# First attention of an attention, gated MLP and attention chain: P of the last sixteen couples of groups turned in blocks on VectorE and put in place through DRAM

## The chip, the cores and the metric

One core of one Trainium2 chip. The time is device time of one launch in microseconds (us), the median of three runs. Engines: PE (TensorE), DVE (VectorE), ACT (ScalarE), POOL (GpSimd) and SP (SyncE, which issues the DMAs here).

## What is computed

Four sequences of 576 positions, fp32 throughout. A first attention (8 heads of 64, a causal window of 64 positions) is followed by a gated MLP (512 to 1024 to 512 with a matmul over positions in the middle), and that by a second, causal attention with four heads, of which a gate picks two per position.

```python
def _attn_ref(q, k, v):                       # q, k, v: (4, 8, 576, 64)
    scores = scale * np.matmul(q, k.transpose(0, 1, 3, 2))
    rel = pos[:, None] - pos[None, :]
    scores = np.where((rel >= 0) & (rel < 64), scores, -1000000000.0)
    attn = np.exp(scores - np.max(scores, axis=-1, keepdims=True))
    attn = attn / (np.sum(attn, axis=-1, keepdims=True) + 1e-09)
    return np.matmul(attn, v)

def _moe_ref(x, w_in, w_spatial, b_spatial, w_out):
    h = np.maximum(x @ w_in, 0.0)
    u, v = h[..., :512], h[..., 512:]
    v_n = (v - mu) / np.sqrt(var + 1e-06)     # over the last axis
    v_s = np.einsum('ts,bsd->btd', w_spatial, v_n) + b_spatial[None, :, None]
    return (u * v_s) @ w_out

def _moe2_ref(x, w_gate, wq, wk, wv, wo):     # four heads, causal
    out += mask[..., None] * w[:, :, kk:kk + 1] * (a @ v @ wo[e])
```

## The kernel before, in words

The program is written out by a planner. The kernel's functions make nodes, each with an engine, a planned duration, what it depends on, which ring slots it takes and which it uses; a node's priority is its entry in the hand-kept list KEY (2089 numbers, in the order in which nodes are made). `Planner.run` (line 224 on) then plays the machine forward: whenever an engine is free, of the nodes that are ready and have room in their rings it starts the one with the lowest priority number, and issues its instructions there and then. So the order on each engine, SP's DMA queue included, is fixed when the program is built, from planned durations. What PE does has a form: 0 for full-size matmuls and transposes, 1 for the scores of the first attention (64x64 pieces of the array), 2 for P times V, 3 for the second attention's scores. Taking a node of form 0 after another form, or the other way round, adds SWITCH to its number in the choice (line 252), and DRAIN (line 187) to its planned time.

There are two stages with one `plan.run()` each. The first makes the first attention and the MLP of all four sequences and folds the MLP's last weight into the weights of the second attention (q, k, v). The second is the second attention.

*The first attention* works in groups: one sequence, one pair of heads, one third of the positions (192). There are 48 groups, taken two at a time by `a_couple(n0)` (24 couples, n0 = 0, 2, ... 46). For one couple:

- SP loads q of each group into a ring of six (`load_q`), and k and v once per pair of heads (`load_kv`). All loads, and the stores of the output, go through `dma` (line 509) onto SP's queue, which takes them strictly in order.
- `s_mm` (form 1): 12 fp32 matmuls (24 instructions) put the scores of three tiles of 64 queries into two PSUM banks, one for each head of the pair; a tile is 128 rows (64 queries of each of the two groups) by 128 keys.
- For each of the two banks: `s_top` (line 629, DVE) adds the mask, scales and takes the row extreme, writing to a tile `pa`; `s_exp` (line 635, ACT) exponentiates; a reduce and a reciprocal (lines 651 and 653, DVE) give 1/sum; `s_norm` (lines 641 on ACT, 643 on DVE or POOL) multiplies; `p_t` (line 647, PE) makes three 128x128 transposes into a PSUM bank; a copy (line 427 on ACT, 431 on DVE) brings them to a tile `pt`. `pa` and `pt` have four buffers each, of one bank's size.
- `pv` (form 2): 12 fp32 matmuls (24 instructions) of v with P from `pt` give the attention's output for both groups in one bank, from which ACT and DVE make a high and a low part (`xh`, `xl`), the operands of the following matmuls in the faster fp32r format. There are six `xh` and six `xl`; a sequence takes four.

*The MLP* of sequence b: `b_v` (V, five pieces of the positions), `b_u` (U, eight pieces), `b_mix` (eight pieces, 14 matmuls each: the matmul over positions). V of a sequence needs `xh` and `xl` of all its heads. While sequence b goes through the MLP, the attention of sequence b+1 is made (`weave`).

*Fillers.* At the start PE has to wait for loads; 60 matmuls of the identity with itself (FILL, `heat`) are nodes of the lowest priority, so they are placed in the first stage wherever nothing else is ready.

*The second attention* (`unit`, line 1278) has its own P, multiplied at line 1317 by DVE or POOL and transposed on PE at line 1329; the change leaves its operations as they are. Every matmul of the program is issued in `mm` (line 416), every copy in `copy` (427 to 431), every subtraction of a high part in `sub` (440).

Of the kernel before, what the change touches and what calls it, by code (L numbers as in the profile page):

```python
# [22 lines left out]
N_XT = 5  # L23
N_VR = 3
N_W2 = 2
N_Q = 6
SWITCH = (51316.5562883, 56444.76665)
A_BIAS = 10098.0
C_BIAS = 162315.0
DVE_BIAS = (924.812225719, 2809.18155958)  # L30
POOL_BIAS = (605.73769693, 3223.06614942)
# [3 lines left out]
EFT = (348.130120865, 591.3127716)  # L35
# [6 lines left out]
    1e+09, 1e+09, 1e+09, 1e+09, 1e+09, 1e+09, 1e+09, 1e+09, 1e+09, 1e+09, 1e+09, 1e+09, 1e+09, -433949.337, -310768.212, -410360.675, -53326.873, -46012.043, -29718.587, 29893.476, 36423.798, 130640.442, 48760.892, -102410.634,  # L42
# [309 lines left out]
def attn_gmlp_moe_kernel(ctx: ExitStack, tc: tile.TileContext, kq0, qT, kT, v, w_in, wspT, b_sp, w_outT,  # L352
# [228 lines left out]
    def a_couple(n0):  # L581
# [42 lines left out]
        for ps, pt in zip(bank, pts):  # L624
# [8 lines left out]
            def s_exp(_, pa=pa, mx=mx):  # L633
                for j in range(3):
                    act.activation(pa[:, j, :], pa[:, j, :], AF.Exp, bias=mx[:, j, 0:1], scale=-1.0,  # L635
                                   accum_out=mx[:, j, 1:2])
# [880 lines left out]
```

## Time and profile before

| what | value |
|---|---|
| runs | 441.45, 441.62, 443.12 us; median 441.62 us |
| the profiled execution | 441.42 us, of which its span (first to last instruction) 439.6 us |
| TensorE clock granted | full (1.00) over the span |
| first stage | to about 258 us |
| instructions | 10921 |
| moved by DMA | 33.11 MB, of which 27.68 MB read from HBM and 4.72 MB written |

The profile is one execution, recorded by the hardware. Busy time of an engine is the time in which an instruction of it was running; matmuls are pipelined, so the duration of one overlaps the next, and what one costs PE is the distance between starts. "Idle before" is the time in which the engine stood before a group's instructions, with what ended it (the releaser). The chain that ended last is followed back from the last instruction, at each step to what released it or to the instruction before it on its engine.

### The profile page before, as it was taken

The numbers are of one execution on the slowest core, as the hardware profiler recorded it, in microseconds if no ns is written. First come the engines' busy times: TensorE is split into PE (matmuls) and PEld (weight loads), VectorE is DVE, ScalarE is ACT, GpSimd is POOL, SyncE is SP. The second block draws the span as 40 slices with busy tenths as digits, with TensorE's granted clock in tenths as the row PEclk, the third lists the DMA queues.
The fourth block names the chain that finished last, engine by engine and source line by source line (L and its number), as shares of the span: only waits on it lengthen the run. The fifth ranks groups of instructions, "written<-read, shape, count | busy, mean of one in ns | idle before, by whom it ended". The sixth has DMA issues, their size and how long they took to land.

```text
span 439.6 us, 10921 instructions
## 1 busy us (share of the span) xinstructions
PE 432.1 (98%) x4058; PEld 390.0 (89%) x4058; DVE 288.6 (66%) x1238; ACT 275.8 (63%) x883; POOL 90.0 (20%) x132
## 2 busy tenths in 40 slices
PE   8999999999999999999999999999999999999997
PEld 7988989998889989998999999999799978987775
DVE  4999998695787583354435444977654956498750
ACT  4899986787785273352433352867576748557873
POOL 4556754121041050001100120120012101110000
PEclk9999999999999999999999999999999999999999
DMA  8995614364145020121001000000020002000114
GB/s 269 339 343 151 238 51 154 96 205 120 38 108 147 1 73 0 49 73 49 1 1 50 0 1 1 0 2 2 1 97 1 1 1 98 1 0 2 49 51 143
DMA packets 31079, 33.11 MB, mean 75 GB/s; under 512 B 1905, under 2 KB 24689, under 8 KB 31026
## 3 DMA queue, kind: packets, MB, share of 16 engines
q1 hardware_dynamic: 31026, 32.41, 23.5%
q8 instruction: 32, 0.52, 0.5%
q14 instruction: 21, 0.17, 0.1%
HBM read 27.68 MB, written 4.72 MB: 74 GB/s over the span
## 4 chain that ended last, share of the span: by engine, by line
PE 84%; DVE 10%; ACT 3%; issue 1%; DMA 1%; POOL 1%; SPq 0%; DVEq 0%; POOLq 0%; ACTq 0%
PE bank L416 75%; PE bank L1329 5%; PE bank L647 4%; DVE p L1307 3%; DVE p L1300 2%; DVE p L1317 1%; ACT p L1313 1%; DMA kt<-in_kT_dram 1%; POOL p L1317 1%; DVE mc L1315 1%; DVE qk L440 0%; DVE mc L1316 0%; ACT pa L635 0%; DVE t2w L440 0%; DVE pa L629 0%
## 5 line engine op out<-in xcount | busy, mean ns | idle before, releaser
L416 PE MATMUL bank<-xh,w 128*128 128x288 f32 x512 | 109.5, 298 | 0.0
L416 PEld LDWEIGHTS bank<-xh,w 128*128 128x128 f32 x512 | 84.1, 188 | 1.4 <-issue 0.3
L416 PE MATMUL bank<-xl,w 128*128 128x288 f32 x256 | 75.5, 295 | 0.0
L416 PE MATMUL bank<-w,xh 128*128 128x512 f32 (+1 forms) x256 | 64.8, 343 | 0.0
L635 ACT ACTIVATE pa<-pa,mx 128x128 f32<-128x128 f32 x144 | 55.8, 393 | 12.7 <-DVE mx L629 12.6
L1313 ACT ACTIVATE p<-p,mc 128x256 f32<-128x256 f32 (+4 forms) x72 | 41.5, 577 | 15.5 <-DVE mc L1307 13.7
L416 PEld LDWEIGHTS bank<-xl,w 128*128 128x128 f32 x256 | 48.1, 188 | 0.4
L416 PEld LDWEIGHTS bank<-w,xh 128*128 128x128 f32 x256 | 43.0, 188 | 5.0 <-DVE mx L651 0.2
L416 PE MATMUL bank<-w,xl 128*128 128x512 f32 (+1 forms) x128 | 43.2, 338 | 0.0
L1317 POOL TENSOR_SCALAR p<-p,mc,fx 128x384 f32<-128x384 f32 (+4 forms) x22 | 14.6, 664 | 133.8 <-DVE mc L1316 66.8
L416 PE MATMUL bank<-wsp_h,vh 128*128 128x288 f32 x128 | 38.9, 304 | 0.0
L416 PE MATMUL bank<-wsp_l,vh 128*128 128x288 f32 x128 | 37.7, 294 | 0.0
L416 PE MATMUL bank<-wsp_h,vl 128*128 128x288 f32 x128 | 37.7, 294 | 0.0
L1307 DVE CUSTOM_DVE_ANT_0 p<-bank,cmask 128x512 f32<-128x512 f32 (+3 forms) x64 | 28.8, 487 | 4.8 <-PE bank L416 2.4
L629 DVE CUSTOM_DVE_ANT_0 pa<-bank,mask 128x128 f32<-128x128 f32 x120 | 28.2, 286 | 4.4 <-PE bank L416 4.3
L853 POOL TENSOR_TENSOR st<-st,nhalf 128x1 f32<-128x1 f32 (+1 forms) x20 | 11.8, 592 | 92.2 <-DVE st L852 56.6
L427 ACT ACTIVATE pg<-bank 128x512 f32<-128x512 f32 (+4 forms) x80 | 29.7, 438 | 0.7 <-PE bank L1329 0.2
L1329 PE MATMUL bank<-ident,p 128*128 128x128 f32 x192 | 27.2, 276 | 1.7 <-DVE p L1317 0.7
L427 ACT ACTIVATE pt<-bank 128x384 f32<-128x384 f32 x41 | 18.4, 486 | 15.8 <-PE bank L647 15.8
L635 ACT ACTIVATION_READ_ACCUMULATOR pa<-pa,mx 128x1 f32 x144 | 27.6, 192 | 0.0
L416 PEld LDWEIGHTS bank<-w,xl 128*128 128x128 f32 x128 | 24.1, 188 | 2.8
L1329 PEld LDWEIGHTS bank<-ident,p 128*128 128x128 f32 x192 | 21.6, 140 | 5.5 <-DVE p L1317 2.6
(193 smaller groups left out, 989.9 us busy)
## 6 DMA issues: line engine op xcount, KB each, us to landing
vt<-in_v_dram SPq DMA_DIRECT2D x12, 512.0 KB, 5.0
qa<-in_qT_dram SPq DMA_DIRECT2D x44, 96.0 KB, 4.4
out_dram<-ot SPq DMA_DIRECT2D x15, 256.0 KB, 2.1
y<-in_w_in_dram SPq DMA_DIRECT2D x7, 512.0 KB, 6.2
kt<-in_kT_dram SPq DMA_DIRECT2D x12, 288.0 KB, 5.3
y<-in_w_outT_dram SPq DMA_DIRECT2D x4, 512.0 KB, 4.2
y<-in_wspT_dram SPq DMA_DIRECT2D x2, 576.0 KB, 4.0
vt<-in_kq_dram SPq DMA_DIRECT2D x2, 384.0 KB, 3.8
```

What stands on the lines that cost most here:

```text
L416: pe.matmul(o, lhsT, rhs, start=start, stop=stop)
L427: act.activation(o, i, AF.Copy)
L629: dve.tensor_tensor_reduce(out=pa[:, j, :], in0=ps[:, j * 128:(j + 1) * 128], in1=mask(j), scale=-0.125, scalar=3.0e38, op0=ALU.add, op1=A ...
L635: act.activation(pa[:, j, :], pa[:, j, :], AF.Exp, bias=mx[:, j, 0:1], scale=-1.0, accum_out=mx[:, j, 1:2])
L647: pe.transpose(ps2[:, j * 128:(j + 1) * 128], pa[:, j, :], ident)
L853: a = N((POOL, 464), lambda e: pool.tensor_tensor(out=st[:m, 9:10], in0=st[:m, 8:9], in1=nhalf[:m], op=ALU.pow), [n1], use=[st])
L1300: dve.tensor_tensor_reduce(out=P[HALF[y], a0:a1], in0=ps[y][HALF[y], :HS], in1=cmask[HALF[y], 0:HS] if i == 0 else tmask[HALF[y]], scale=- ...
L1307: tops = [N((DVE, t_tt(L)), lambda _, ps=ps: dve.tensor_tensor_reduce(out=P[:, cs], in0=ps[:, cs], in1=cmask[:, 512 - L:512], scale=-0.125 ...
L1313: a = N((ACT, 284 + 0.87 * L), lambda e: act.activation(P[:, cs], P[:, cs], AF.Exp, bias=mc[:, 0:1], scale=-1.0, accum_out=mc[:, 2:3]), to ...
L1315: a = N((DVE, 70), lambda e: dve.tensor_scalar(mc[:, 3:4], mc[:, 2:3], 1e-9, None, op0=ALU.add), [a], use=[mc], prio=prio)
L1317: a = N({POOL: 328 + 0.832 * L, DVE: 90 + 0.52 * L}, lambda e: engs[e].tensor_scalar(P[:, cs], P[:, cs], mc[:, 3:4], fx[:, I, ev:ev + 1], ...
L1329: pe.transpose(ps[:, j * m:(j + 1) * m], P[:, c0 + j * 128:c0 + (j + 1) * 128], ident)
```

## The change

`N_DT = 16` splits the couples. Those with n0 below 16 (eight couples) keep the way described above. For the other sixteen:

- `s_top`, `s_exp` and `s_norm` write `pa` in another order of columns: four blocks of 32 keys, in each both heads, the three tiles and 32 keys. `pa` now holds both banks of a couple (768 columns, four buffers).
- `p_t` and the copies out of PSUM are not made. Instead one DVE instruction, `dve.transpose` of 128x768 in place, turns each block of 32x32; it waits for the norms of both banks.
- Four DMAs, one for each 32 partitions (98 KB), store the result to a DRAM tile `dr` (a ring of four). One DMA of 393 KB, after all four have landed, loads it with the blocks in place into `pt` (768 columns, three buffers). Both move rows of 192 numbers (768 bytes). All are on SP's queue.
- `pv` reads P from `pt` in two runs of 32 columns.

Beside that, PE's planned times of forms 1 and 2 are without the cost of the form change, which is now in the table DRAIN, with a form 4 of its own for transposes; SWITCH multiplies DRAIN in the choice instead of standing alone; the biases (DVE_BIAS, POOL_BIAS, EFT) and one planned time of the second stage (line 1317 on DVE) are other numbers. Per changed couple four nodes go and three come, so KEY has 2073 entries instead of 2089, and all but the first 61 (the warm-up and the fillers) are new numbers. FILL stays at 60. The list KEY is left out here:

```diff
+N_DT = 16
...
-SWITCH = (51316.5562883, 56444.76665)
+SWITCH = (508440.848706, 1241.9455123)
 A_BIAS = 10098.0
 C_BIAS = 162315.0
-DVE_BIAS = (924.812225719, 2809.18155958)
-POOL_BIAS = (605.73769693, 3223.06614942)
+DVE_BIAS = (1446.55002243, 5820.53335932)
+POOL_BIAS = (791.503455194, 4103.69459824)
...
 WARM = 8
 FILL = 60
...
-EFT = (348.130120865, 591.3127716)
+EFT = (590.178157957, 3173.43987937)
...
-    DRAIN = (0.0, 145.0, 145.0, 92.0), (0.0, -78.0, 0.0, 0.0), (0.0, 0.0, -78.0, 0.0), (0.0, 0.0, 0.0, -92.0)
+    DRAIN = ((0.0, 138.0, 137.0, 191.0, 0.0),
+             (212.0, 0.0, 158.0, 212.0, 165.0),
+             (204.0, 151.0, 0.0, 204.0, 157.0),
+             (194.0, 141.0, 140.0, 0.0, 147.0),
+             (0.0, 145.0, 144.0, 198.0, 0.0))
...
-                    key = n.prio + (SWITCH[self.phase] if e == PE and (n.form > 0) != (self.form > 0) else 0.0), n.nth
+                    key = n.prio + (SWITCH[self.phase] * self.DRAIN[self.form][n.form] if e == PE else 0.0), n.nth
...
+    dram = ctx.enter_context(tc.tile_pool(name="dram", bufs=1, space=bass.MemoryType.DRAM))
...
-    r_pa = ring(p1, "pa", [128, 3, 128], F32, 4)
+    r_pa = ring(p1, "pa", [128, 768], F32, 4)
 
     r_mx = fixed(MX)
-    r_pt = ring(p1, "pt", [128, 3, 128], F32, 4)
+    r_pt = ring(p1, "pt", [128, 768], F32, 3)
+    r_dr = ring(dram, "dr", [4, 4, 32, 192], F32, 4)
...
-        pts = [r_pt.new(), r_pt.new()]
+        far = n0 >= N_DT
+        pa, pt = r_pa.new(), r_pt.new()
+
+        def at(j, e):
+            if far:
+                return pa.t.rearrange("p (k e j c) -> p k e j c", k=4, e=2, j=3)[:, :, e, j, :]
+            return pa[:, e * 384 + j * 128:e * 384 + (j + 1) * 128]
+
+        def sq(x):
+            return x.rearrange("p (k c) -> p k c", c=32) if far else x
+
+        def prob(j, x, e):
+            if far:
+                return pt.t.rearrange("p (i e j c) -> p i e j c", i=4, e=2, j=3)[:, 2 * x:2 * x + 2, e, j, :]
+            return pt[:, e * 384 + j * 128 + x * 64:e * 384 + j * 128 + x * 64 + 64]
...
-        S_N[n0] = S_N[n0 + 1] = top = N((PE, 816), s_mm, kn + [Q_N[n0], Q_N[n0 + 1], S_N.get(n0 - 1)], alloc=bank, use=hk, prio=prio,
+        S_N[n0] = S_N[n0 + 1] = top = N((PE, 654), s_mm, kn + [Q_N[n0], Q_N[n0 + 1], S_N.get(n0 - 1)], alloc=bank, use=hk, prio=prio,
                                         form=1)
-        done = []
-        for ps, pt in zip(bank, pts):
-            pa, mx, ps2 = r_pa.new(), r_mx.new(), r_at.new()
-
-            def s_top(_, ps=ps, pa=pa, mx=mx):
+        done, first, turned = [], [], []
+        for e2, ps in enumerate(bank):
+            mx = r_mx.new()
+
+            def s_top(_, ps=ps, e2=e2, mx=mx):
                 for j in range(3):
-                    dve.tensor_tensor_reduce(out=pa[:, j, :], in0=ps[:, j * 128:(j + 1) * 128],
-                                             in1=mask(j), scale=-0.125, scalar=3.0e38,
+                    dve.tensor_tensor_reduce(out=at(j, e2), in0=sq(ps[:, j * 128:(j + 1) * 128]),
+                                             in1=sq(mask(j)), scale=-0.125, scalar=3.0e38,
                                              op0=ALU.add, op1=ALU.min, accum_out=mx[:, j, 0:1])
 
-            def s_exp(_, pa=pa, mx=mx):
+            def s_exp(_, e2=e2, mx=mx):
                 for j in range(3):
-                    act.activation(pa[:, j, :], pa[:, j, :], AF.Exp, bias=mx[:, j, 0:1], scale=-1.0,
+                    act.activation(at(j, e2), at(j, e2), AF.Exp, bias=mx[:, j, 0:1], scale=-1.0,
                                    accum_out=mx[:, j, 1:2])
 
-            def s_norm(e, pa=pa, mx=mx):
+            def s_norm(e, e2=e2, mx=mx):
                 if e == ACT:
                     for j in range(3):
-                        act.activation(pa[:, j, :], pa[:, j, :], AF.Copy, scale=mx[:, j, 3:4])
+                        act.activation(at(j, e2), at(j, e2), AF.Copy, scale=mx[:, j, 3:4])
+                elif far:
+                    o = pa.t.rearrange("p (k e j c) -> p k e j c", k=4, e=2, j=3)[:, :, e2]
+                    engs[e].tensor_tensor(out=o, in0=o, in1=mx[:, None, :, 3:4].to_broadcast([128, 4, 3, 32]), op=ALU.mult)
                 else:
-                    engs[e].tensor_tensor(out=pa.t, in0=pa.t, in1=mx[:, :, 3:4].to_broadcast([128, 3, 128]), op=ALU.mult)
-
-            def p_t(_, pa=pa, ps2=ps2):
-                for j in range(3):
-                    pe.transpose(ps2[:, j * 128:(j + 1) * 128], pa[:, j, :], ident)
-
-            a = N((DVE, 606), s_top, [top], alloc=[pa, mx], use=[ps], prio=prio)
+                    o = pa[:, e2 * 384:(e2 + 1) * 384].rearrange("p (j c) -> p j c", j=3)
+                    engs[e].tensor_tensor(out=o, in0=o, in1=mx[:, :, 3:4].to_broadcast([128, 3, 128]), op=ALU.mult)
+
+            a = N((DVE, 606), s_top, [top] + first, alloc=[mx] + ([] if e2 else [pa]), use=[ps] + ([pa] if e2 else []), prio=prio)
+            first.append(a)
             a = N((ACT, 1160), s_exp, [a], use=[pa, mx], prio=prio)
             a = N((DVE, 75), lambda e, mx=mx: dve.tensor_reduce(out=mx[:, :, 3], in_=mx[:, :, 1:3], axis=AX.X, op=ALU.add),
                   [a], use=[mx], prio=prio)
             a = N((DVE, 91), lambda e, mx=mx: dve.reciprocal(mx[:, :, 3], mx[:, :, 3]), [a], use=[mx], prio=prio)
             a = N({POOL: 1053, DVE: 450, ACT: 880}, s_norm, [a], use=[pa, mx], prio=prio, sbuf=True)
-            a = N((PE, 327), p_t, [a], alloc=[ps2, pt], use=[pa], prio=prio)
-            done.append(N(on_copy(384), lambda e, pt=pt, ps2=ps2: copy(e, pt.t.rearrange("p a b -> p (a b)"), ps2[:, :384]),
+            if far:
+                done.append(a)
+                continue
+            ps2 = r_at.new()
+
+            def p_t(_, e2=e2, ps2=ps2):
+                for j in range(3):
+                    pe.transpose(ps2[:, j * 128:(j + 1) * 128], at(j, e2), ident)
+
+            a = N((PE, 327), p_t, [a] + turned, alloc=[ps2] + ([] if e2 else [pt]), use=[pa] + ([pt] if e2 else []), prio=prio, form=4)
+            turned.append(a)
+            done.append(N(on_copy(384), lambda e, e2=e2, ps2=ps2: copy(e, pt[:, e2 * 384:(e2 + 1) * 384], ps2[:, :384]),
                           [a], use=[ps2, pt], prio=prio))
+        if far:
+            a = N((DVE, 870), lambda e: dve.transpose(pa.t, pa.t), done, use=[pa], prio=prio, sbuf=True)
+            dr = r_dr.new()
+
+            def there():
+                for i in range(4):
+                    dma(dr[i].rearrange("k a w -> a k w"), pa[i * 32:(i + 1) * 32, :].rearrange("p (k w) -> p k w", k=4))
+
+            a = load(128 * 3072, 4, there, [a], alloc=[dr], use=[pa], prio=prio)
+            done = [load(128 * 3072, 1, lambda: dma(pt.t.rearrange("p (i w) -> p i w", i=4),
+                                                    dr.t.rearrange("i k a w -> (k a) i w")), [a], alloc=[pt], use=[dr], prio=prio)]
...
-                        mm(ps3[HALF[e], (3 * x + j) * 64:(3 * x + j + 1) * 64], vap(x, vi, e), pts[e][:, j, HALF[x]])
+                        mm(ps3[HALF[e], (3 * x + j) * 64:(3 * x + j + 1) * 64], vap(x, vi, e), prob(j, x, e))
...
-        o = N((PE, 848), pv, done + [PV_N.get(k[:2]) for k in grp] + vn, alloc=[ps3] + new, use=pts + hv, prio=prio,
+        o = N((PE, 699), pv, done + [PV_N.get(k[:2]) for k in grp] + vn, alloc=[ps3] + new, use=[pt] + hv, prio=prio,
...
-        a = N({POOL: 328 + 0.832 * L, DVE: 90 + 0.52 * L}, lambda e: engs[e].tensor_scalar(
+        a = N({POOL: 328 + 0.832 * L, DVE: 190 + 0.52 * L}, lambda e: engs[e].tensor_scalar(
...
-    nc = _bacc.Bacc("TRN2", target_bir_lowering=False, num_devices=1)
+    nc = _bacc.Bacc("TRN2", target_bir_lowering=False, num_devices=1, dynamic_dma_scratch_size=2048)
```

## Rows read from the trace of the kernel before

**Rows 1.** The page's first part: busy time, share of the span, instructions.

```profile
PE 432.1 (98%) x4058; PEld 390.0 (89%) x4058; DVE 288.6 (66%) x1238; ACT 275.8 (63%) x883; POOL 90.0 (20%) x132
```

**Rows 2.** Busy time by stage: us, each engine, clock, DMA share, GB/s.

```profile
28.00:66.00 38.00, 37.00 (x444) 32.42 (x446) 35.35 (x133) 35.93 (x115) 24.53 (x26) 1.00 0.52 175
66.00:100.00 34.00, 34.00 (x413) 32.03 (x406) 27.58 (x138) 25.69 (x104) 9.97 (x12) 1.00 0.48 147
100.00:150.00 50.00, 50.00 (x546) 44.97 (x545) 34.33 (x159) 32.04 (x121) 8.98 (x13) 1.00 0.33 91
150.00:200.00 50.00, 50.00 (x506) 46.29 (x505) 26.80 (x99) 25.30 (x82) 7.27 (x8) 1.00 0.15 43
```

**Rows 3.** The chain that ended last, merged, in order: start, duration in us.

```profile
60.16 15.97 PE bank L416 x190
76.13 1.31 PE bank L647 x12
...
196.21 0.33 PE bank L647 x3
196.53 77.48 PE bank L416 x592
```

**Rows 4.** PE's timeline at the ninth couple's scores: start, duration in us.

```profile
42.38 0.89 PE L416 MATMUL bank<-kt,qa 64*64 64x128 f32 x24
```

**Rows 5.** Groups of instructions by shape, copies of P: busy us, mean ns.

```profile
L427 ACT ACTIVATE pt<-bank 128x384 f32<-128x384 f32 x41 | 18.4, 486 | 15.8 <-PE bank L647 15.8
...
L431 DVE COPY pt<-bank 128x384 f32<-128x384 f32 x7 | 3.8, 545 | 0.0
```

**Rows 6.** The same view, DVE from SBUF to SBUF.

```profile
L440 DVE TENSOR_TENSOR xl<-y,xh 128x576 fp32r<-128x576 f32 x10 | 7.9, 813 | 3.6 <-ACT xh L427 3.4
...
L1317 DVE TENSOR_SCALAR p<-p,mc,fx 128x576 f32<-128x576 f32 x7 | 4.0, 578 | 0.1
...
L440 DVE TENSOR_TENSOR w<-vt,w 128x1024 fp32r<-128x1024 f32 x3 | 3.7, 1226 | 1.1 <-ACT w L427 0.9
```

**Rows 7.** DMA: queue and issues, 66 to 200 us; the page's stores.

```profile
q1 hardware_dynamic: 16206, 11.47, 29.4%
...
L509 SPq DMA_DIRECT2D qa<-in_qT_dram x23: 327/423/1668, 67.4 to 132.5; - x23
...
DMA to landing us min/median/max: 1.9/4.1/6.8
...
out_dram<-ot SPq DMA_DIRECT2D x6, 128.0 KB, 2.3
```

**Rows 8.** ACT's timeline, the last exp of two couples: start, duration in us.

```profile
142.81 0.19 ACT L635 ACTIVATION_READ_ACCUMULATOR pa<-pa,mx 128x1 f32 x1
...
192.36 0.19 ACT L635 ACTIVATION_READ_ACCUMULATOR pa<-pa,mx 128x1 f32 x1
```

**Rows 9.** PE's timeline, blocks of PV and what follows them.

```profile
87.64 0.92 PE L416 MATMUL bank<-pt,vt 128*64 128x64 f32 x24
88.48 0.89 PE L416 MATMUL bank<-kt,qa 64*64 64x128 f32 x24
...
177.64 1.62 PE L416 MATMUL bank<-pt,vt 128*64 128x64 f32 x48
179.19 0.40 PE L416 MATMUL bank<-wsp_h,vh 128*128 128x288 f32 x1
...
198.31 0.92 PE L416 MATMUL bank<-pt,vt 128*64 128x64 f32 x24
```

**Rows 10.** PE's timeline, fillers at the end of the first stage.

```profile
256.02 2.84 PE L416 MATMUL bank<-ident 128*128 128x128 f32 x24
```

**Rows 11.** Waits of PE's weight loads: total us, times, longest.

```profile
PEld bank L1329 <- DVE p L1317: 2.6, 7, 0.7
PEld bank L1329 <- POOL p L1317: 1.5, 4, 0.6
```

More of the change, by code (lines that the diff above doesn't have):

```diff
@@ L41 @@
     1e+09, 1e+09, 1e+09, 1e+09, 1e+09, 1e+09, 1e+09, 1e+09, 1e+09, 1e+09, 1e+09, 1e+09, 1e+09, 1e+09, 1e+09, 1e+09, 1e+09, 1e+09, 1e+09, 1e+09, 1e+09, 1e+09, 1e+09, 1e+09,
-    1e+09, 1e+09, 1e+09, 1e+09, 1e+09, 1e+09, 1e+09, 1e+09, 1e+09, 1e+09, 1e+09, 1e+09, 1e+09, -433949.337, -310768.212, -410360.675, -53326.873, -46012.043, -29718.587, 29893.476, 36423.798, 130640.442, 48760.892, -102410.634,
[85 rows of a table removed]
+    1e+09, 1e+09, 1e+09, 1e+09, 1e+09, 1e+09, 1e+09, 1e+09, 1e+09, 1e+09, 1e+09, 1e+09, 1e+09, -1183064.921, -1180401.788, -984440.607, -770425.267, -965452.953, -700022.553, -767274.631, -735858.745, -731589.461, -769196.477, -803420.559,
[84 rows of a table added]
 )
@@ L914, in gv @@
         def gv(g):
-            return g.t.rearrange("p a b -> p (a b)")[:, :HS]
+            return g[:, :HS]
         def gate(o):
@@ L1253, in scores @@
                 ps = [r_sc.new(), r_sc.new()]
-                a = N((PE, 92 + 3 * t_mm(HS)), lambda _, ps=ps, i=i: three(
+                a = N((PE, 3 * t_mm(HS)), lambda _, ps=ps, i=i: three(
                     [p[:, :HS] for p in ps], (S - 64, S - 128), i * HS, (i + 1) * HS),
@@ L1269, in go @@
                 c += w
-        a = N((PE, 92 + sum(3 * t_mm(128 * I + 128) for I in tiles)), go, deps, alloc=ps + pp + gets, use=[qk], prio=prio, form=3)
+        a = N((PE, sum(3 * t_mm(128 * I + 128) for I in tiles)), go, deps, alloc=ps + pp + gets, use=[qk], prio=prio, form=3)
         started(a)
@@ L1336, in unit @@
         f, an = a, PG_N[key][:1]
-        a = N((PE, nj * 109), tr, [f] + an, alloc=[ps], use=[P], prio=prio)
+        a = N((PE, nj * 109), tr, [f] + an, alloc=[ps], use=[P], prio=prio, form=4)
         a = N(on_copy(nj * m, 1), tc_, [a], use=[ps, pg], prio=prio)
@@ L1344, in unit @@
             a = N((PE, 109), lambda _: pe.transpose(pt[:64, :128], P[:, 512:576], ident), [f] + PG_N[key][:1], alloc=[pt],
-                  use=[P], prio=prio)
+                  use=[P], prio=prio, form=4)
             a = N(on_copy(128), lambda e_: copy(e_, pg[HALF[hb], 3, :, 64 * hb:64 * hb + 64],
@@ L1372, in c_pv @@
         cs = slice(i0, i0 + 256)
-        o = N((PE, 800 if grp == 0 else 2200), go, PG_N[b, pr, grp] + V2_N[b] + (VT_N[b] if grp else []) + ([] if new else O_N[b, pr][:1]),
+        o = N((PE, 651 if grp == 0 else 2056), go, PG_N[b, pr, grp] + V2_N[b] + (VT_N[b] if grp else []) + ([] if new else O_N[b, pr][:1]),
               alloc=[ps] + new, use=[pg, v2] + ([vt] if grp else []), prio=prio, form=2)
@@ L1417, in c_wo @@
             return
-        a = N((PE, 78 + 6 * t_mm(512)), lambda e: mm3(ps.t, [
+        a = N((PE, 6 * t_mm(512)), lambda e: mm3(ps.t, [
             ((part(0, pr), part(1, pr)), (view(wh.t)[:, pr, :], view(wl.t)[:, pr, :])) for pr in range(2)]),
```

169 rows, old and new, of the table KEY are left out of this document.

## The prediction

> **What bounds the kernel now.** I read the page first, then the stages, then the chain that ended last. PE is busy 98% of the span, the other engines 20 to 66% [rows 1]. The mean hides where a second engine is close: from 28 to 66 us DVE works 35.35 of 38 us, from 66 to 200 us 88.7 of 134 us (27.58 + 34.33 + 26.80), while PE has no idle time that the rows show after 66 us [rows 2]. The chain says what this means: from 60.16 us to 274 us it holds nothing but PE, line 416 (all matmuls) and line 647 (the transposes of P) by turns [rows 3]. In that stretch a microsecond taken from PE is a microsecond of the kernel, as long as nothing else comes late. Before 60 us the chain also runs through DMA, ACT and DVE, and there the change removes nothing: the eight couples that keep their transposes are scored up to 41 us, and the ninth, the first that changes, at 42.38 us [rows 4].
>
> **The change, part by part.**
>
> *Transposes off PE.* Sixteen couples times two halves times three are 96 transposes. The chain from 60 us on has exactly these: 18 pieces of line 647 with 96 instructions, 10.97 us together; the first has twelve in 1.31 us and the last three in 0.33 us, so about 0.11 us each [rows 3]. Term: **-11.0 us**. The PV matmul then reads P in two runs of 32 columns instead of 64 in one; no row shows such an operand, and I price it at nothing: the same 64 columns are streamed; both ends lie inside the switch term's bounds below.
>
> *Copies out of PSUM.* 32 of 48 go: ACT has 41 at 486 ns and DVE the other 7 at 545 ns [rows 5]. So ACT loses some 27 x 0.486 = 13 us and DVE some 5 x 0.545 = 2.5 us. Neither is on the chain after 60 us: 0.
>
> *Turning on VectorE.* Sixteen DVE transposes of 768 columns. No row shows one. Nearest are SBUF to SBUF operations: 813 ns for 576 columns, 1226 ns for 1024, both with two inputs, and 578 ns for 576 columns with one input [rows 6]. Interpolating the first pair gives 0.99 us for 768; the ends are 0.58 and 1.23. I take 0.99, as the transpose lies in width between that pair: 15.8 us of DVE, 13.3 net of the copies. From 66 to 200 us that makes 102 us out of some 123: 83%, room enough, so 0 on the chain. In front of it in DVE's order stand the norms of both halves; queued behind a waiting transpose are the next couples' score reads and the splits of x, which free PSUM banks for PE. The Trainium skill ("VectorE: DVE Perf Modes", The three transpose paths) gives 311 ns for a 128x128 bf16 turn on VectorE, which scaled to six such tiles is an estimate of 1.87 us, or 29.9 us in all. By it DVE would stand at 95% from 66 to 200 us and the sum would carry a DVE wait; no run here shows it yet.
>
> *Through DRAM and back.* Each couple adds four stores and one load on SP's queue: 80 issues. An issue takes 0.33 to 0.42 us [rows 7], together some 34 us of SP, behind which the loads of q, k and v for later couples stand. These have a lead of three couples (QA holds six groups), and S1 of the couple that needs them would be the one to wait. On the DMA engines 80 transfers are 16384 packets of 768 B; 16206 packets took 29.4% of 16 engines over 134 us [rows 7], 39 ns each, so 40 us are added to 39 of 123: 64%. No bound. (The smaller scratch space for dynamic DMAs in the diff's last line is priced at nothing: the rows show the loads on a hardware queue.) What counts is latency. After the turn: three issues (1.3), the fourth to its landing 2.3 (the stores of the output, the only writes to DRAM shown), then the load, 4.1 from issue to landing (1.9 to 6.8) [rows 7], with 0.99 for the turn 8.7 us. The old way is 0.33 us of transposes and 0.49 of copy, with the handoffs some 1.2 us [rows 3, 5]. So each P comes **some 7.5 us later** (5 to 10 by the two ends of the landing).
>
> *What covers that.* In the present order I measured, for all sixteen couples, from the last exp to the first PV matmul. The new way needs about 9.9 us there (0.9 to 1.2 for the norm as before, 8.7). Eleven couples have 10.9 to 34.6 us (the longest from 143.00 to 177.64); five have less: 5.8 (the last couple, 192.55 to 198.31), 7.0, 7.6, 9.7 and 9.8 [rows 8, 9]. Together they lack 9.6 us. Most of it PE can fill with other matmuls; the cover is the mix, U and V work that stands on both sides. In front of each batch's V it runs short. I take **+2.0 us**, bounds 0 and 9.6. P's ring grows from two couples to three and the ring in front of it from two to four, which helps.
>
> *The order.* All 2073 priorities differ, and what a change of PE's form costs in the choice is now weighed by the gap that the form change takes, so heavily in the first stage (508441 x 138 against 51317) that PE stays in one form while it can. The trace has 44 blocks of such work: 24 of scores, each one couple long, and 20 of PV, four of them with two couples. A pair of PV takes 1.55 us (177.64 to 179.19), a single one 0.84 (87.64 to 88.48) [rows 9]: 0.13 us per block merged. Blocks of two everywhere are 20 fewer (2.6 us), blocks of four 32 fewer (4.2 us). The eight banks stand against it, since scores take two per couple. I take 15 fewer: **-2.0 us**, bounds 0 and -4.2.
>
> *Fillers.* FILL stays at 60; only the list of priorities is 16 entries shorter. Twelve fillers stand at the end of the first stage, 24 matmuls from 256.02 us for 2.8 us [rows 10]; I expect the same, bounds -2.8 and, should the start idle less and leave twice as many, +2.8.
>
> *Second stage.* It is only reordered. Its weight loads wait for DVE and POOL 2.6 + 1.5 us in front of the transposes of line 1329 [rows 11]. That could go or double: bounds -4.1 and +4.1, value 0.
>
> Sum: -11.0 + 2.0 - 2.0 = -11.0. The profiled execution took 441.42 us (span 439.6 and 1.8 around it), 0.2 below the median of 441.62, so the median comes to about **430.5 us**.
>
> **The rivals.**
>
> *Longer blocks and a better order* pay fully: -11.0 - 4.2 - 2.8 and +1 for waits for P: 424. For it: the weight on form changes. Against: PSUM banks.
>
> *Part of the gain goes back*, in waits for P or on DVE. The stretch from 28 to 66 us has only 2.65 us of DVE free [rows 2], and up to three changed couples may turn there: 3 x 0.99 = 3.0 us; or the shortfalls of 9.6 us are covered only in half, 4.8. Together -11.0 - 2.0 + 7.8: 436.
>
> *P through DRAM is the new bound, and the kernel is slower.* The place is the start of each batch's V (batches 1 to 3), where V needs x of all heads. If PE has run out of mix and U by then, it stands for the whole 7.5 us three times, 22.5 us; with no merged blocks 441.6 - 11.0 + 22.5 = 453. It decides from 13 us of such waits on (11.0 + 2.2). For it: the last couple is the tightest of all, and batch 3's V waits for it. Against: four couples fit in the first ring, and eleven of sixteen now have longer than the way takes. The Trainium skill ("VectorE: DVE Perf Modes", Rules for kernel authors) speaks for this rival: it sends a 128x128 transpose to TensorE where PSUM will do and keeps VectorE for turns within a block of 32; no run here shows the other way yet.
>
> *The change doesn't act*: P lands early, but the removed PE time returns as idle PE in the second stage, whose start at 258 us hangs on the folded weights. Their matmuls are on the PE chain too [rows 3], so I give it little: 441.
>
> **How the numbers follow.** A difference of 0.5% (2.2 us) is about what a measurement of this kernel can tell from none. Forecast near 430.5: 0.47. Better order, near 424: 0.18. Partly given back, near 436: 0.19. No change: 0.05. Slower: 0.11. Faster is the sum of the first three less a small tail, 0.83; same 0.06; slower 0.11. The range leaves out the slower case, part of the unchanged one and the best of the second: 422.5 to 439.5.
>
> **What would show it.** Right: line 647 has 48 matmuls instead of 144; PE's first stage ends 9 to 13 us earlier; ACT loses 13 us; a DVE transpose of 128x768 near 1 us, sixteen times; 64 stores and 16 loads with 768 B packets; the chain from 60 us on still PE alone; fewer, longer blocks of kt,qa and pt,vt. Wrong: waits of PE's weight loads for a DMA on pt of over 5 us in total, a DVE share over 90% from 66 to 190 us, or a second stage longer than before.

## The result and the profile after

The changed kernel takes 436.58 us in the median (435.34 to 437.01), the kernel before 442.25 on the same chip; the ratio is 0.9867, 95% interval 0.9836 to 0.9898. The forecast was 430.5 us with a range to 439.5: the sign is right, the gain about half of the 11 us that were expected. The profiled execution of the changed kernel took 436.34 us with a span of 434.6; against the span before of 439.6 us that is 5.0 us, and the readings below explain these 5.0.

The page's first part, to be held against [rows 1]: TensorE (PE) has lost 10 us, ScalarE 10, VectorE 5, and GpSimd has gained 25, because it does more of the splits and norms in the new order.

```profile
PE 422.0 (97%) x3962; PEld 380.2 (87%) x3962; DVE 283.6 (65%) x1205; ACT 265.9 (61%) x870; POOL 115.4 (27%) x176
```

The stages (us, then busy time of PE, PEld, DVE, ACT and POOL, granted clock, DMA share, GB/s), against [rows 2]. The stretch from 28 to 66 us is the one that got worse: PE 34.74 of 38 us where it had 37.00, and a clock of 0.96. From 100 us on PE is full, as before; DVE stays under 70% there.

```profile
28.00:66.00 38.00, 34.74 (x388) 29.71 (x387) 29.62 (x144) 34.50 (x132) 22.19 (x25) 0.96 0.61 189
66.00:100.00 34.00, 32.94 (x407) 30.44 (x406) 30.52 (x118) 28.23 (x101) 12.55 (x16) 1.00 0.77 222
100.00:150.00 50.00, 50.00 (x555) 46.04 (x554) 33.13 (x148) 27.20 (x109) 15.35 (x18) 1.00 0.67 195
150.00:200.00 50.00, 50.00 (x490) 45.88 (x489) 28.25 (x107) 22.57 (x78) 13.55 (x18) 1.00 0.54 144
```

The operations of the new route, in the groups by shape (count, then busy us and mean ns) and in the DMA issues (KB each, us from issue to landing). The transposes of P are 48 where 144 were; the turn on VectorE took 0.97 us where the steps had 0.99 [rows 6]; ScalarE copies P 15 times in place of 41 [rows 5]; the store lands after 2.5 us and the load after 3.9 us, where 2.3 and 4.1 were taken [rows 7].

```profile
L683 PE MATMUL bank<-ident,pa 128*128 128x128 f32 x48 | 7.7, 276 | 1.4 <-POOL pa L667 1.4
...
L690 DVE STREAM_TRANSPOSE pa<-pa 128x768 f32<-128x768 f32 x16 | 15.4, 970 | 2.5 <-ACT pa L661 2.3
...
L432 ACT ACTIVATE pt<-bank 128x384 f32<-128x384 f32 x15 | 6.7, 475 | 1.0 <-PE bank L683 1.0
...
dr<-pa SPq DMA_DIRECT2D x64, 96.0 KB, 2.5
pt<-dr SPq DMA_DIRECT2D x16, 384.0 KB, 3.9
```

The chain that ended last, merged (start, duration in us), against [rows 3]. Before, it was PE alone from 60.16 us on. Now it runs on through ScalarE, VectorE and pieces of three trips of P by way of DRAM (a store, a load of another couple, a store and a load of a third), and comes back to PE at 93.14 us. At the end of the first stage it leaves PE once more, for GpSimd.

```profile
63.26 1.19 ACT pa L655 x7
69.69 4.20 DMA dr<-pa
75.58 1.19 ACT pa L655 x6
77.79 1.16 ACT pa L655 x6
79.40 6.71 DMA pt<-dr
86.13 3.43 DMA dr<-pa
89.68 3.33 DMA pt<-dr
93.14 155.09 PE bank L421 x1440
248.80 1.28 POOL xh L434 x2
```

That chain looks worse than it is. PE's timeline (start, duration, what ended the idle time ahead of it) has one wait for P in the whole kernel, 1.06 us. It also shows where the blocks stand: here scores and PV alternate one couple at a time, as before [rows 9].

```profile
88.68 0.92 PE L421 MATMUL bank<-pt,vt 128*64 128x64 f32 x24
89.53 0.89 PE L421 MATMUL bank<-kt,qa 64*64 64x128 f32 x24
90.35 0.92 PE L421 MATMUL bank<-pt,vt 128*64 128x64 f32 x24
91.20 0.89 PE L421 MATMUL bank<-kt,qa 64*64 64x128 f32 x24
...
93.14 0.92 PE L421 MATMUL bank<-pt,vt 128*64 128x64 f32 x24 [1.06 <-DMA pt<-dr]
```

**Where the gain went.** I counted the matmuls that PE had started by a given time and gave each kind one price in both kernels (512 columns 0.233 us, 288 columns 0.133, a couple's scores 0.82, its PV 0.80), leaving out transposes of P and fillers. That is the work that both kernels must do:

| us of such work done by | 50 us | 66 | 100 | 150 | 200 | 250 |
|---|---|---|---|---|---|---|
| before | 27.1 | 40.7 | 70.7 | 115.9 | 162.7 | 212.8 |
| after | 19.9 | 34.8 | 66.7 | 116.3 | 166.1 | 216.2 |

From 50 to 250 us the changed kernel does 196.3 us of it and the kernel before 185.7: the 10.6 us that the transposes were to give are there (with a wait of about 1 us in either kernel in that stretch, for P after the change and for a norm at 59.6 us before it). But at 50 us, when not one P has gone the new way, it is 7.2 us behind. After 250 us it gains another 1.6. So -10.6 + 7.2 - 1.6 = -5.0.

The groups of PE's matmuls up to 50 us show what is missing, before and after. Before:

```profile
L416 PE MATMUL bank<-ident 128*128 128x128 f32 x112 | 16.7, 303 | 1.5 <-DVE ident L446 1.5
L416 PE MATMUL bank<-w,xh 128*128 128x512 f32 x32 | 10.2, 399 | 0.0
L416 PE MATMUL bank<-w,xl 128*128 128x512 f32 x16 | 6.3, 393 | 0.0
...
L416 PE MATMUL bank<-xh,w 128*128 128x288 f32 x19 | 4.4, 305 | 0.0
```

After:

```profile
L421 PE MATMUL bank<-ident 128*128 128x128 f32 x136 | 20.0, 298 | 1.5 <-DVE ident L451 1.5
L421 PE MATMUL bank<-w,xh 128*128 128x512 f32 x18 | 5.8, 404 | 0.0
...
L421 PE MATMUL bank<-kt,qa 64*64 64x128 f32 x120 | 5.6, 307 | 1.7 <-DVE mx L674 1.6 <-DVE mx L649 0.2
...
L421 PE MATMUL bank<-w,xl 128*128 128x512 f32 x8 | 3.1, 391 | 0.0
```

48 products of the V blocks have become 26, U has not begun, and 24 more filler products ran, since all 60 fillers are now used before 38 us (2.7 us at 0.11 each); of [rows 10] nothing is left at the boundary. PE's timeline shows the rest: two waits, of 1.44 and 1.57 us, and a block of scores that takes 1.68 us where it takes 0.89 otherwise.

```profile
40.53 0.88 PE L683 MATMUL bank<-ident,pa 128*128 128x128 f32 x6 [1.44 <-POOL pa L667]
42.97 1.68 PE L421 MATMUL bank<-kt,qa 64*64 64x128 f32 x24 [1.57 <-DVE mx L674]
44.58 1.55 PE L421 MATMUL bank<-pt,wol 128*64 128x64 f32 x24
46.06 0.89 PE L421 MATMUL bank<-kt,qa 64*64 64x128 f32 x24
```

The first wait ends with a norm on GpSimd. For the second the profile names line 674, VectorE's reciprocal, but the last one had ended at 42.00 us. What came just before 42.97 was a load of k: SP issued it at 39.11 us, behind four loads of q, and it landed 3.8 us later, at 42.88. PE's first weight load of these scores began 0.06 us after that landing, and it did so in all seven profiles that have this wait in the new order, with landings from 41.73 to 42.89 us. So the second wait is one for SP's queue, not for VectorE. SP's timeline, and the time to landing:

```profile
39.11 0.43 SPq L515 DMA_DIRECT2D kt<-in_kT_dram  x1
DMA to landing us min/median/max: 3.8/3.8/3.8
```

The windows say why the block behind it is slow: the granted clock is 0.50 from 42.6 to 46 us, the level of 1.2 GHz, after 3.6 us in which PE worked 0.96.

```profile
39.00:42.60 3.60, 0.96 (x10) 0.64 (x6) 3.60 (x25) 3.60 (x18) 2.23 (x4) 1.00 0.75 196
42.60:46.00 3.40, 3.03 (x48) 2.67 (x48) 1.54 (x11) 0.90 (x5) 1.46 (x2) 0.50 0.33 100
```

**The boundary between the stages** is a second place that no step of the prediction had. PE ends the first stage at 252.8 us and waits 2.62 us for GpSimd's copies of zt. GpSimd's own timeline shows a queue: it stands until 248.35 us at a memset of pg, then splits two channels (L434, L445), and only then turns to zt.

```profile
248.35 0.45 POOL L1102 MEMSET pg<- 64x128 f32 x2 [7.78 <-PE bank L421]
248.78 1.31 POOL L434 TENSOR_SCALAR xh<-y 128x576 fp32r<-128x576 f32 x2
250.05 2.81 POOL L445 TENSOR_TENSOR xl<-y,xh 128x576 fp32r<-128x576 f32 x2
252.93 0.45 POOL L1102 MEMSET pg<- 64x128 f32 x2
253.37 0.25 POOL L434 TENSOR_SCALAR zt<-xh 128x64 fp32r<-128x64 f32 x1
```

### The profile page after: what moved, and what is told of

It reads as the page before. It is cut to its first block, busy times and chain, and to the rows that moved or that the text cites. A ratio compares the mean times of both kernels' runs of the same rounds, so it can differ in the third digit from the quotient of the medians.

```text
span 434.6 us, 10940 instructions
## 1 busy us (share of the span) xinstructions
PE 422.0 (97%) x3962; PEld 380.2 (87%) x3962; DVE 283.6 (65%) x1205; ACT 265.9 (61%) x870; POOL 115.4 (27%) x176
## 4 chain that ended last, share of the span: by engine, by line
PE 77%; ACT 8%; DMA 5%; DVE 5%; POOL 2%; issue 2%; SPq 0%; POOLq 0%; ACTq 0%; DVEq 0%
PE bank L421 72%; PE bank L1371 5%; ACT pa L655 3%; DMA pt<-dr 2%; DMA dr<-pa 2%; DMA y<-in_w_in_dram 1%; ACT pa L661 1%; DVE pa L649 1%; ACT bank L804 1%; DVE p L1349 1%; ACT xh L432 1%; DVE p L1342 1%; ACT pt L432 0%; POOL zt L434 0%; POOL xl L445 0%
## 5 line engine op out<-in xcount | busy, mean ns | idle before, releaser
L421 PE MATMUL bank<-xh,w 128*128 128x288 f32 x512 | 110.9, 299 | 0.0
L655 ACT ACTIVATE pa<-pa,mx 128x128 f32<-128x128 f32 x144 | 55.9, 396 | 4.9 <-DVE mx L649 4.8
L1355 ACT ACTIVATE p<-p,mc 128x384 f32<-128x384 f32 (+4 forms) x72 | 41.6, 579 | 20.2 <-DVE mc L1349 19.1
L1359 POOL TENSOR_SCALAR p<-p,mc,fx 128x128 f32<-128x128 f32 (+4 forms) x31 | 19.4, 632 | 120.0 <-ACT p L1355 28.2
L421 PE MATMUL bank<-wsp_h,vh 128*128 128x288 f32 x128 | 37.9, 296 | 0.0
L432 ACT ACTIVATE pg<-bank 128x512 f32<-128x512 f32 (+4 forms) x80 | 30.6, 442 | 1.5 <-PE bank L1371 1.0
L432 ACT ACTIVATE xh<-bank 128x192 fp32r<-128x192 f32 (+1 forms) x35 | 12.4, 380 | 22.7 <-PE bank L421 22.7
L661 ACT ACTIVATE pa<-pa,mx 128x128 f32<-128x128 f32 x69 | 22.6, 393 | 5.6 <-DVE mx L674 4.5
L421 PE MATMUL bank<-qk 64*128 64x288 f32 (+4 forms) x288 | 25.4, 319 | 0.0
```

The costliest lines, as they stand in the source:

```text
L421: pe.matmul(o, lhsT, rhs, start=start, stop=stop)
L432: act.activation(o, i, AF.Copy)
L655: act.activation(at(j, e2), at(j, e2), AF.Exp, bias=mx[:, j, 0:1], scale=-1.0, accum_out=mx[:, j, 1:2])
L661: act.activation(at(j, e2), at(j, e2), AF.Copy, scale=mx[:, j, 3:4])
L1355: a = N((ACT, 284 + 0.87 * L), lambda e: act.activation(P[:, cs], P[:, cs], AF.Exp, bias=mc[:, 0:1], scale=-1.0, accum_out=mc[:, 2:3]), to ...
L1359: a = N({POOL: 328 + 0.832 * L, DVE: 190 + 0.52 * L}, lambda e: engs[e].tensor_scalar(P[:, cs], P[:, cs], mc[:, 3:4], fx[:, I, ev:ev + 1], ...
```

## The experiments

Theory A: the route is worth the time of its transposes, and the new order of the first 50 us gives 7 us back. The rivals: the route itself gives it back, in waits for P or on VectorE (B); or until some 95 us the other engines feed PE no faster, so that an early start only moves the waits (C). To change one thing at a time, each kernel below takes its steps from a fixed list (SEQ) instead of from the planner; with the changed kernel's own list it is the changed kernel, engine by engine.

**The old route in the new order.**

```
-N_DT = 16
+N_DT = 99
 SEQ: per couple of the last 16
-    turn, store, load
+    p_t, copy, p_t, copy
```

> The new order of every engine is kept, and the last 16 couples go the old way again: 96 transposes on TensorE and 32 copies out of the banks on ScalarE or VectorE, no turn, no store, no load. Theory A (the transposes lie on TensorE's path for their whole length, some 10.5 us, and what the changed kernel lacks of that is lost by the new order): 446 to 448 us, the first stage 10 to 12 us longer than in the changed kernel. Rival B (the order is as good as the old one and the new route is worth only the 5.7 us that were measured, because its waits give the rest back): 441 to 443 us.

Measured: 445.58 us, ratio to the kernel before 1.0068 (1.0041 to 1.0095), 0.4 us below A's range and 2.6 above B's. The route is worth 0.9867 / 1.0068 = 0.980, some 9 us, and the new order by itself makes the old route slower by 3 us. By 250 us this kernel has done 207.0 us of work, 9.2 less than the changed one. That is nearly 96 x 0.11 = 10.6 us less the 1.06 us wait for P, which this kernel doesn't have. A holds, B falls. Part of the 3 us is the clock: its three runs with a mean granted clock of 1.000 took 442.95 to 443.98 us, the three with 0.996 444.51 to 446.49, the four with 0.991 or 0.992 446.59 to 446.86; all runs of the kernel before have 0.999 or 1.000. In its profile, one of those with 0.992, the clock falls twice, each time for 3.41 us.

**The old start with the new rest.**

```
 SEQ = (steps that began before 50 us in the kernel before, in its order)
     + (all others, in the new order)
-N((PE, 228.0), lambda e: heat(1), ...)
+N((PE, 228.0), (lambda e: heat(1)) if _ < 48 else (lambda e: None), ...)
```

> The changed kernel, whose steps are issued in the order of the kernel before as far as they began before 50 us there, and after that in the new order; the last 12 fillers issue nothing. The new route is untouched, since no couple that uses it is ready by then. Theory A (the 7 us that TensorE is behind at 50 us are lost for good, since it is busy from 60 us on): 429 to 432 us. Rival C (the early V blocks are paid for by later score reads and splits, so that TensorE waits between 50 and 80 us instead): 436 to 440 us.

Measured: 437.47 us, ratio 0.9899 (0.9863 to 0.9935): no better than the change. It is level with the kernel before at 50 us (27.2 us of work done), and at 100 us about with the changed one (67.3 against 66.7). PE's timeline shows where that went, in two waits that name score reads on VectorE; the granted clock fell behind the second.

```profile
58.34 0.40 PE L365 MATMUL bank<-xh,w 128*128 128x288 f32 x1 [2.80 <-DVE mx L593]
73.90 1.55 PE L365 MATMUL bank<-pt,vt 128*64 128x64 f32 x24 [2.19 <-DVE mx L593]
```

Rival C holds for this list.

**The first 27 to 58 us sorted anew**, copies and subtractions of x ahead of the splits of w_in (the same list otherwise):

> The changed kernel, with the steps that begin between 27 and 58 us sorted anew so that the copies and subtractions of the first two sequences' x come before the splits of w_in, and the V block (L897's stream) no longer waits: second V block near 40 us in place of 46.9. Theory A: 431 to 434 us, the idle stretch of TensorE at 39 to 43 us and the lower clock behind it gone. Rival C (other engines set the pace up to 60 us, the idle time only moves): 435.5 to 437 us.

Measured: 437.54 us, ratio 0.9892 (0.9855 to 0.9928). 36 V products stand by 50 us instead of 26, and the clock is 1.00 from 28 to 50 us. But a wait of 1.89 us for P has come at 74.75 us, with a fall of the clock, and 66.3 us of work are done by 100 us against 66.7. The time is 0.5 us above C's range and far from A's: C again, as far as the time goes.

**GpSimd's order at the boundary.**

```
 SEQ, second stage, GpSimd first:
-memset pg, xh, xh, xl, xl, memset pg, 12 steps of zt
+xh, xh, xl, xl, 12 steps of zt, memset pg, memset pg
```

> The changed kernel, with GpSimd's first steps of the second stage in another order: the xh and xl of two channels first, then the twelve zt copies, and the two memsets of pg last. Theory D (the 2.6 us that TensorE waits between the stages are GpSimd's queue: it sits behind the memset until 248.35 us, and its xl then holds VectorE's last xl): the wait shrinks to under 0.5 us and the time is 433.5 to 434.5 us. Rival (the second stage is set by a chain of its own that starts elsewhere, or the memory of zt comes free only then): 436 to 437 us.

Measured: 431.78 us, ratio 0.9768 (0.9734 to 0.9802), 4.8 us below the change. GpSimd's timeline has the splits in what was idle time and zt at 248.14 us, and PE starts on zt at 251.56 without a wait:

```profile
239.46 1.52 POOL L378 TENSOR_SCALAR xh<-y 128x576 fp32r<-128x576 f32 x2
240.94 3.80 POOL L389 TENSOR_TENSOR xl<-y,xh 128x576 fp32r<-128x576 f32 x2
248.14 0.24 POOL L378 TENSOR_SCALAR zt<-xh 128x64 fp32r<-128x64 f32 x1 [3.39 <-DVE pa L904]
```

Theory D holds and was too modest: its range ended at 433.5. Against the changed kernel's profile the span is 4.4 us shorter, and only part of that is D's: 1.1 because no P is waited for in this execution (67.8 us of work by 100 us against 66.7), 3.3 at the boundary (by 258 us 225.4 against 221.0, less the 1.1). The wait for P belongs to the execution and not to this edit, since up to the boundary every engine has the same order in both. The clock adds to the gain in some runs: behind the 2.6 us wait it fell for 3.41 us in seven of the eight profiles that keep the new order's boundary, and the changed kernel's own is the one without. Its four runs all have a mean granted clock of 0.996, as its profiled one with its single fall at 42.6 us; the four runs here have 0.995, 1.000, 0.996 and 1.000, so two of them have one fall less, 1.7 us at half the clock.

**The waits at 39 to 43 us filled.**

```
 SEQ: fillers 60 and 55 moved ahead of the steps that wait
-lambda e: heat(1)
+lambda e, n=6 if _ in (54, 59) else 1: heat(n)
```

> The kernel of the run that reorders GpSimd at the stage boundary (431.8 us), with two of the 60 fillers moved into TensorE's two waits at 39 and 41.4 us and made six products long each. Theory E (the lower clock from 42.6 to 46.0 us follows from these two waits and costs some 1.7 us): the granted clock stays at 1.00 from 40 to 48 us and the time is 429.5 to 430.7 us. Rival (the fillers delay the transposes and scores behind them by as much): 431.5 to 432.5 us.

Measured: 433.4 us, ratio 0.981 (0.978 to 0.984). The clock stayed at full, and at 66 us the kernel is 1.4 us ahead of the run before (36.2 against 34.8); at 100 us it is behind (67.4 against 67.8), with a wait of 1.7 us for P. The first half of theory E holds, its price doesn't: what the filled waits gave was lost again in a wait for P. Whether the fillers brought that wait is open, since it comes and goes between executions of one order (1.06 us in the changed kernel, none in the run before this one).

**P without the trip.**

```
-return pt.t.rearrange(...)
+return pa.t.rearrange(...)
-for i in range(4): dma(dr[i]..., pa[...])
+pass
-lambda: dma(pt.t..., dr.t...)
+lambda: None
-r_pa = ring(p1, "pa", [128, 768], F32, 4)
+r_pa = ring(p1, "pa", [128, 768], F32, 6)
```

> The changed kernel without the stores and loads of P: the PV products of the last 16 couples read the turned blocks where they lie in pa, which has two more buffers. Left out: the moving of the blocks into place, so the output is not the reference's. Theory A (the trip through DRAM costs the one wait that the trace shows, 1.1 us): 435 to 436 us. Rival (the trip holds more back than that, through SyncE's queue and through the couples' order): 431 to 434 us.

Measured: 436.39 us, ratio 0.9879 (0.9852 to 0.9907). Its profile has no wait for P and one fall of the clock more than that of the change. That hides the gain: its four runs have a mean granted clock of 0.991 or 0.992, the changed kernel's four 0.996. By 250 us it has done 217.4 us of work, 1.2 more than the changed kernel, which is A's wait; the rival falls.

**Without turn and trip** (as above, and the turn's step issues nothing):

> As the run without the trip, and without VectorE's 16 turns too (15.4 us of VectorE). Left out: turning and moving P, so the output is not the reference's. Theory A (VectorE has room for the turns): within 1 us of the run without the trip, 434 to 436 us. Rival (VectorE sets the pace between 50 and 95 us, where TensorE gets ahead no faster than before the change): 3 us or more below it, 430 to 432.5 us.

Measured: 435.43 us, ratio 0.9879 (0.9832 to 0.9927). From 66 to 250 us it does 182.4 us of work, the run without the trip 182.6, the changed kernel 181.4. So VectorE has room for the turns, and all that the new route still costs in this order is about 1 us.

**The same with the old start:**

> The run with the start of the kernel before (437.5 us), and there too P is neither turned nor moved. Left out: turning and moving P, so the output is not the reference's. Theory F (the old start cannot be had with the new route, because the route wants scores early; the waits at 58 and 74 us are its price): 429 to 432 us. Rival C (those waits come from the score reads and splits that VectorE does later in this order, whatever the route): 435 to 438 us.

Measured: 434.96 us, ratio 0.985 (0.9821 to 0.9878). Two waits for score reads are still there, 2.09 us at 57.5 and 1.49 at 73.0, though no P travels; 2.5 us less than the run with the trip. The time is at the lower edge of C's range (434.96 against 435) and 3 us above F's.

**Old start, sorted again over 26 to 75 us, with the new boundary** (the edits of the second and the fourth run together, and a list in which, by the planner's own costs, PE never waits):

> The new route with the order of the kernel before up to 50 us, the steps from 26 to 75 us sorted again so that TensorE is never without work there, 12 fillers left out, and GpSimd's steps at the stage boundary as in the run of 431.8 us. Theory G (the 7 us that the new order loses before 50 us belong to that order and not to the route; sorted with care, the old start and the new route go together): 425 to 429 us. Rival C (score reads, splits and the P trip feed TensorE no faster up to 95 us, and waits take the place of the late start): 431 to 434 us.

Measured: 431.78 us, ratio 0.979 (0.9766 to 0.9814), the same as with the boundary alone. 25.4 us of work are done by 50 us (19.9 there) and 67.8 by 100 us (67.8 there). The windows of this kernel, and below of the one with the boundary alone, show the busiest engine beside PE: VectorE, 68.11 of 72 us here.

```profile
28.00:100.00 72.00, 66.74 (x786) 57.97 (x785) 68.11 (x275) 53.59 (x198) 42.90 (x44) 1.00 0.69 211
```

```profile
28.00:100.00 72.00, 69.03 (x802) 61.38 (x801) 60.61 (x263) 63.46 (x235) 34.71 (x40) 0.98 0.71 209
```

The time is in C's range and G falls. C's mechanism is not shown by it: of PE's five waits from 40 to 82 us, 3.3 us in all, four (2.8 us) name VectorE and one a load of P, which fits, but no run gave VectorE less to do in this list.

**The new boundary in the kernel before:**

> The kernel before, old route and old order, with only the stage boundary changed: GpSimd does the xh and xl of two channels and the zt copies before the two memsets of pg, and the last 12 fillers, which stood in the 2.6 us between the stages there, issue nothing. Theory D (the wait between the stages has nothing to do with the change): 438.5 to 440 us, 2 to 3 us less than the kernel before. Rival (before, the zt copies wait for something else, since they are on ScalarE there): 441 to 443 us.

Measured: 445.73 us, ratio 1.0092 (1.0062 to 1.0123): 4 us slower than the kernel before, outside both ranges. The list gave GpSimd the splits and the copies of zt, which ScalarE and VectorE do for the most part in the kernel before. GpSimd has a piece of the first stage's x to subtract at 255.00 us, the splits come behind it, zt only from 259.80 to 262.8, PE waits 3.4 us, and the clock falls behind the wait. So this list does not carry the gain over to the old order; whether another one could use the time of the twelve fillers there was not tried. In the new order GpSimd is idle from 240.6 to 248.35 us, and there the splits found their place.

**Half of the change.** N_DT = 26, with transposes and copies put back for five couples:

> The changed kernel, in which only the last 11 couples go the new way (N_DT 26) and the five before them, whose PV stood at 74 to 112 us, are transposed on TensorE again: 30 of the 96 transposes come back, 3.3 us at 0.11 us each, every engine's order else kept. Theory A (TensorE is the bound from 45 us on in the changed kernel): 439 to 440 us. Rival C (up to 95 us the other engines and the P trips feed TensorE, so that time saved there is worth little): 436 to 437.5 us.

Measured: 438.49 us, ratio 0.9936 (0.9913 to 0.9958), between the two. By 250 us it has done 214.0 us of work, 2.2 less than the changed kernel. That is 3.3 us of transposes less the 1.06 us wait for P, which is gone from this profile and which I had left out of A's figure. So in the new order PE's time counts in the stretch where these couples stand, and A holds with that correction.

**Fillers in the wait at the boundary.**

```
+for _ in range(16 if b == 0 else 0):
+    mm(ps[:, :128], ident, ident)
 mm3(ps[:, :260], ...)
```

> The changed kernel with 16 more filler products ahead of the first matmul that reads zt, so that TensorE is busy for some 2 us of the 2.6 us in which it waits between the stages. Theory H (the wait itself is set by GpSimd and stays, but a fall of the granted clock behind it, 3.4 us at the lower level in the runs that show it, goes): 435 to 436 us, granted clock 1.00 from 250 to 262 us in every run. Rival (the fillers run late and hold the products behind them up): 437 to 438.5 us.

Measured: 435.7 us (434.0 to 440.44), ratio 0.9891 (0.9853 to 0.9928). In its profile the clock is full from start to end, at 42 us as well, and the span is 432.2 us. H's median holds; the interval is too wide to tell it from the change. Nor did the clock stay at full in every run, as H wanted: its mean is 1.000 in three of the six, 0.996 in two and 0.988 in one. The fillers ran from 250.07 to 253.56 us, so the boundary took 0.7 us longer than with the wait, and the shorter span of the profile does not come from them: it is 2.1 us ahead at 50 us already, where the order is the changed kernel's and the load of k landed at 41.73 us instead of 42.88.

## Why the prediction was right, and where it was off

*Transposes off PE, -11.0.* Right: 10.6 us between 50 and 250 us with the wait for P already in it, and 9.2 by the run with the old route. *Copies, 0, and turning, 0.* Right: 0.97 us a turn against 0.99, and without turn and trip the kernel gains 1 us. The estimate that scaled the Trainium skill's 311 ns ("VectorE: DVE Perf Modes", The three transpose paths) to 1.87 us was twice too long for this 128x768 turn, and VectorE stood at 69% from 66 to 200 us (91.9 of 134), not at 95%.

*Waits for P, +2.0.* Right in kind, 1.06 us. The trip itself was longer than worked out: from the end of the turn to the landing 7.2 to 14.0 us in the sixteen couples, 10.0 in the median, where the steps had 7.7 (the trace has ten of the landings; the other six, the shortest trip among them, are put at the median 3.9 us behind the issue). The new order covers it by scoring earlier: between landing and PV lie 0.1 to 12.9 us.

*Longer blocks, -2.0.* Wrong: there are 24 blocks of scores, each one couple long, and 21 of PV, where there were 24 and 20. The larger weight on form changes merged nothing on balance. What I had read from the diff as an intent was not in the program.

*The step that failed* is the one about the time before 60 us: "there the change removes nothing". It removes nothing there, but it reorders, and of a list in which every priority differs I had priced only the blocks. The new order has 7.2 us less done at 50 us: 2.7 of fillers, 3.0 of waits and 1.7 of lower clock are 7.4, and three transposes fewer by then give 0.3 back. Half of the waits is for a load of k that stands behind four loads of q on SP's queue. *Fillers, 0*, was wrong with it: the twelve that stood at the boundary now run at the start, and having the lowest priority they too mark time in which the plan had nothing else for PE.

*Second stage, 0.* It gains 1.6 us, inside the bounds. The place where it could have gained more was in the trace: the twelve fillers [rows 10] may mark a time in which PE had nothing else to do, and I only asked how many they would be.

*The signs and the range.* The first stage's work on PE ends 3.4 us earlier (252.8 us against 256.2), not 9 to 13; ScalarE loses 10 us, not 13; the chain is not PE alone from 60 us on; and the blocks did not merge. None of the three signs of being wrong came. That the time lies in the range is in part luck: the upper end of the range was kept for waits for P and for VectorE, and what filled it was a late start that no term had.

*The rivals.* "Partly given back, 436" has the right time by the wrong mechanism: waits for P and VectorE's load cost 1 us together, not 7.8. "P through DRAM is the bound" is refuted: with the transposes on TensorE the same order takes 445.58 us. TensorE is where the Trainium skill ("VectorE: DVE Perf Modes", Rules for kernel authors) puts a 128x128 transpose whose result may lie in PSUM; in this kernel, where PE is the bound for most of the time and VectorE is not, the runs go the other way by 9 us.

What stays open: whether some order has both the old start and the new route. Three other starts were tried, one of them also without turn and trip, and had 66.3 to 69.6 us of work done by 100 us; the kernel before had 70.7, and 33 more transposes of P than the changed kernel (81 against 48). In the best sorted of them VectorE is 95% busy up to there, which fits C; in the spliced one it is 87% (62.33 of 72 us), and no run took work off VectorE with the sorted start. That VectorE is the cause was not shown; SP's queue is a rival, since one wait of the new start is its load of k. The best time, 431.78 us, is that of the change with GpSimd's order at the boundary, with or without the sorted start.

## What to carry to other kernels

Where a change comes with a new order, price the order by itself: count what the bounding engine has done by a few fixed times, before and after, and ask of each stretch whether that engine was the bound there. A filler that stands in a wait hides the wait; look behind it. Where the profile names a releaser that had ended long before, look for the load that landed just then. Work that a queue does early because it was written first (a memset, a split) can hold up the one copy that the next stage starts with.

## What was not expected of the hardware

- The granted clock fell from full (2.4 GHz) to 0.50 (1.2 GHz) for 3.41 us at a time, behind waits of PE of 1.4 and 1.6 us close together, of 1.9, of 2.2 or of 2.6 us, and not each time: behind one of 2.80 us in the run with the old start it didn't, nor behind the 2.6 us at the boundary in the changed kernel's profile. At 0.50 a block of scores took 1.68 us instead of 0.89. With PE kept at work by fillers in a wait the clock stayed at full in both profiles that tried it, but not in all runs of the two kernels.
- A subtraction of 128x288 on VectorE took 3.61 us from 249.57 us on, while GpSimd split two channels from SBUF to SBUF until 252.86 us; with GpSimd's splits moved away the same one took 0.46.
- A turn of 128x768 in fp32 took VectorE 0.97 us, 1.3 ns a column.
- P's way through DRAM took 7 to 14 us for 384 KB, of which the two landings are 2.5 and 3.9 us in the median; the rest passes on SP's queue. One load of P, for instance, was issued at 89.68 us, 0.12 us after its last store had landed.
